# Attention and a two-layer MLP on one core: the first scores of batch 1 set between two begun blocks, and the last 128 tokens stored by column pieces on two queues

## The chip, the cores and the metric

One core of one Trainium2 chip. The metric is the device time of one execution in microseconds (us).

Names: PE is TensorE's matmul unit, PEld its weight loads, DVE is VectorE, ACT ScalarE, POOL GpSimd, SP SyncE. A q behind a name is that engine's sequencer. PSUM is the memory that matmuls write, in banks. A DMA is a transfer between memories; an engine issues it, and here it has landed when its semaphore, a counter that other instructions wait for, has its full count in the trace.

## The reference

```python
q, k, v: (8, 12, 448, 64)                      # batch, heads, tokens, head size, float32
attn = softmax(q @ k^T / 8) @ v                # per head
x    = attn.transpose(0, 2, 1, 3).reshape(3584, 768)
h    = leaky_relu(x @ w_in, 0.01)              # 768 -> 2048
out  = h @ w_out                               # 2048 -> 768, float32, 11 MB
```

## The kernel before

Heads are worked in pairs; HP = 6 pairs make one batch. The first batch's six pairs are the opening. In the main loop, PE alternates between MLP blocks of batch i and attention clusters of later batches. A turn lies between the two: it begins two blocks of the first MLP layer (`part` for m = 0 and 1) with the four pairs of heads that are done, and finishes them when the last pairs are transposed.

```python
def part(i, m, kks, bank=None):        # some of the 6 matmuls of one 128x384 block of x @ w_in
    ...
    for kk in kks:
        nc.tensor.matmul(open_t[m][:, :n], w_in_sb[:, kk, ts(m, P)], xT[:, kk, at:at + n],
                         start=(fresh and kk == kks[0]), stop=(kk == KD - 1))

def pv(u, j, bank=None):               # 16 matmuls of one head, then on DVE:
    ...
    nc.vector.reciprocal(rec, ps[:SC, :, D:])
    nc.vector.tensor_mul(x_t[u][:, :, j, :], ps[:SC, :, :D], rec.to_broadcast([SC, NSC, D]))

# the turn
a, b = idle_slot()                     # two PSUM banks of the scores' pool
part(0, 0, range(4), a)
part(0, 1, range(4), b)
x_transposes(HP - 2)                   # 4 PE transposes of x, then a DVE copy to xT
scores(HP, 0)                          # 2 matmuls, one per head, 64 rows each
expo(HP, 0)                            # exponential on ACT
scores(HP, 1)
expo(HP, 1)
part(0, 0, (4,))
part(0, 1, (4,))
pv(HP - 1, 0)
pv(HP - 1, 1)
scores(HP, 2)
expo(HP, 2)
x_transposes(HP - 1)
transposes(HP + 1)                     # 8 PE transposes of q and k
...                                    # mlp(0) begins with part(0, 0, (5,)) and part(0, 1, (5,))

# the second MLP layer, for each 128 tokens c and each half w of the 768 columns
for m in range(MD):                    # 16 matmuls of 384 columns
    nc.tensor.matmul(ps[:, :NW], h[:, m, ts(c, P)], w_out_sb[:, m, ts(w, NW)], ...)
nc.vector.tensor_copy(o[c][:, ts(w, NW)], ps[:, :NW])
if w == 1:
    store(o.pop(c), cuts[i] + c * P)   # the last 128 tokens: 16 rows, then 112 rows, both by SyncE
```

The softmax here doesn't subtract the row's maximum and nothing guards it: scores larger than these inputs give would overflow.

## Time and profile before

| | before |
|---|---|
| time, median of three runs | 419.16 us (418.84, 419.16 and one of 1447.26) |
| span of the profiled execution | 416.76 us |
| opening: up to the first block matmul of the turn | 26.48 us |
| turn: from there to the first of the last block matmuls | 5.273 us |
| middle: from there to the end of the last matmul | 379.98 us |
| end: from there to the end of the span | 5.02 us |

The four stretches add up to the span. They are taken from the start and end times of PE's instructions in the trace; a matmul's end is modelled, which does not matter where the same instruction is compared. The profile lines of the turn and of the end are in the prediction.

### The profile page before, as it was taken

How to read it: one execution, taken by the hardware profiler on the slowest of the kernel's cores; microseconds unless marked ns; L12 is line 12 of the kernel's file. 1: busy time of each engine (PE TensorE's matmuls, PEld its weight loads, DVE VectorE, ACT ScalarE, POOL GpSimd, SP SyncE). 2: the span in 40 equal slices, each digit the busy share in tenths (PEclk: the TensorE clock that was granted, in tenths of full speed). 3: DMA queues.
4: the chain of work that ended last, by engine and by line, in shares of the span. 5: the costliest groups of instructions: out<-in, count | busy, mean ns of one | idle time of the engine just before them, and what ended most of it. 6: DMA issues, size and time to landing. Idle time of an engine off the chain costs nothing.

```text
span 416.8 us, 8966 instructions
## 1 busy us (share of the span) xinstructions
PE 407.5 (98%) x3742; PEld 235.2 (56%) x3742; DVE 103.5 (25%) x294; ACT 228.9 (55%) x324; POOL 105.1 (25%) x177
## 2 busy tenths in 40 slices
PE   7999999999999999999999999999999999999995
PEld 2566665544656665654565656554465656654562
DVE  3652433211223113320232212221132212310021
ACT  5988872567434774476633684467643486214200
POOL 8876655311112213130311311131130100000000
PEclk9999999999999999999999999999999999999999
DMA  9999999981666848594466947767365521130022
GB/s 137 192 202 203 202 200 122 213 196 40 177 173 172 173 107 187 138 213 110 115 161 175 203 103 188 184 153 185 91 157 137 125 43 24 50 88 0 0 77 76
DMA packets 96265, 57.23 MB, mean 137 GB/s; under 512 B 53216, under 2 KB 92640, under 8 KB 96224
## 3 DMA queue, kind: packets, MB, share of 16 engines
q1 hardware_dynamic: 76592, 44.17, 43.8%
q0 software_dynamic: 19392, 12.26, 20.5%
q8 instruction: 29, 0.48, 0.5%
q10 hardware_dynamic: 240, 0.23, 0.2%
q14 instruction: 12, 0.10, 0.1%
HBM read 45.61 MB, written 11.01 MB: 136 GB/s over the span
## 4 chain that ended last, share of the span: by engine, by line
PE 95%; DVE 2%; DMA 1%; issue 0%; POOLq 0%
PE mm L343 35%; PE mm L314 35%; PE pv L258 13%; PE sc L237 10%; PE tr L222 2%; DMA fq<-in_q_dram 1%; DVE x L266 1%; PE tr L279 1%; PE sc L314 1%; DVE o L347 0%; DVE qkT L226 0%; DVE rec L265 0%; PE mm L177 0%; DVE qkb L137 0%; DVE xT L280 0%
## 5 line engine op out<-in xcount | busy, mean ns | idle before, releaser
L246 ACT ACTIVATE e<-sc 112x896 bf16<-112x896 f32 x192 | 164.7, 915 | 100.8 <-PE sc L237 100.4
L343 PE MATMUL mm<-w_out_sb,h 128*128 128x384 bf16 x896 | 150.2, 326 | 0.5 <-DVE x L266 0.2
L314 PE MATMUL mm<-xT,w_in_sb 128*128 128x512 bf16 (+1 forms) x756 | 148.6, 353 | 0.2 <-DVE x L266 0.2
L343 PEld LDWEIGHTS <-h 128*128 128x128 bf16 x896 | 85.9, 98 | 55.5 <-issue 0.5
L314 PEld LDWEIGHTS <-w_in_sb 128*128 128x128 bf16 x768 | 72.9, 98 | 66.2 <-issue 1.2
L329 ACT ACTIVATE h<-mm 128x512 bf16<-128x512 f32 (+1 forms) x126 | 68.7, 545 | 58.7 <-PE mm L314 58.6
L258 PEld LDWEIGHTS <-e 112*128 112x128 bf16 x1536 | 56.5, 98 | 25.6 <-issue 16.5
L139 POOL CAST v<-fv 112x512 bf16<-112x512 f32 x30 | 18.5, 616 | 194.0 <-PE pv L258 181.7
L258 PE MATMUL pv<-v,e 112*128 112x65 bf16 x1536 | 65.2, 194 | 0.0
L347 DVE COPY o<-mm 128x384 f32<-128x384 f32 x56 | 31.2, 557 | 133.9 <-PE mm L343 133.9
L265 DVE RECIPROCAL rec<-pv 112x4 f32<-112x4 f32 x96 | 17.5, 182 | 150.1 <-PE pv L258 149.6
L237 PE MATMUL sc<-qkT 64*128 64x448 bf16 x384 | 49.8, 357 | 0.7 <-DVE qkT L226 0.7
L266 DVE TENSOR_TENSOR x<-pv,rec 112x256 bf16<-112x256 f32 x96 | 40.7, 424 | 3.3
L237 PEld LDWEIGHTS <-qkT 64*128 64x128 bf16 x384 | 13.8, 94 | 18.8 <-issue 9.9
L137 POOL CAST qkb<-fq 112x512 bf16<-112x512 f32 x30 | 18.4, 613 | 1.8 <-issue 1.2
L137 POOL CAST qkb<-fk 112x512 bf16<-112x512 f32 x30 | 18.4, 613 | 0.9 <-DMA fk<-in_k_dram 0.8
L139 POOL COPY v<-fv 112x512 bf16<-112x512 bf16 x17 | 10.4, 617 | 10.4 <-DMA fv<-in_v_dram 5.7
L137 POOL COPY qkb<-fq 112x512 bf16<-112x512 bf16 x14 | 8.7, 620 | 12.3 <-DMA fq<-in_q_dram 12.3
L226 DVE COPY qkT<-tr 128x896 bf16<-128x896 bf16 (+1 forms) x15 | 8.8, 588 | 11.2 <-PE tr L222 11.2
L137 POOL COPY qkb<-fk 112x512 bf16<-112x512 bf16 x14 | 8.7, 618 | 4.3 <-DMA fk<-in_k_dram 4.3
L222 PE MATMUL tr<-ident,qkb 112*128 112x112 bf16 x112 | 8.8, 225 | 0.3 <-DVE qkb L137 0.3
L222 PEld LDWEIGHTS <-qkb 112*128 112x128 bf16 x112 | 7.2, 103 | 2.7 <-ACT qkb L188 0.6
(30 smaller groups left out, 51.6 us busy)
## 6 DMA issues: line engine op xcount, KB each, us to landing
fk<-in_k_dram SPq DMA_DIRECT2D x31, 224.0 KB, 3.4
fq<-in_q_dram SPq DMA_DIRECT2D x30, 224.0 KB, 3.2
fv<-in_v_dram SPq DMA_DIRECT2D x30, 224.0 KB, 3.8
w_in_sb<-in_moe_w_in_dram POOLq DMA_DIRECT2D x4, 768.0 KB, 11.7
w_out_sb<-in_moe_w_out_dram POOLq DMA_DIRECT2D x4, 768.0 KB, 13.6
out_dram<-o SPq DMA_DIRECT2D x8, 336.0 KB, 3.3
out_dram<-o SPq DMA_DIRECT2D x8, 288.0 KB, 2.6
out_dram<-o SPq DMA_DIRECT2D x8, 240.0 KB, 3.4
```

Source lines behind the costliest of these rows:

```text
L137: by(qk_sb[u][:, x].rearrange("p so h d -> p h so d"), f)
L139: by(v_sb[u % NV][:, :, :, :D], f)
L222: nc.tensor.transpose(tr[:, i, ts(so, SC)], qk_sb[u][:, i, so], ident[:SC, :SC])
L237: nc.tensor.matmul(ps[:, j, :S], t[j * D:(j + 1) * D, S + c * SC:S + c * SC + P], t[j * D:(j + 1) * D, :S], start=True, stop=True,)
L246: nc.scalar.activation(e[:, :, c, :], sc_t.pop((u, c))[:SC, :, :S], AX.Exp, scale=scale)
L258: nc.tensor.matmul(ps[:, qc, :], e[:, at:at + P], vt[:, j, c, :], start=(c == 0), stop=(c == NSC - 1),)
L265: nc.vector.reciprocal(rec, ps[:SC, :, D:])
L266: nc.vector.tensor_mul(x_t[u][:, :, j, :], ps[:SC, :, :D], rec.to_broadcast([SC, NSC, D]))
L314: nc.tensor.matmul(open_t[m][:, :n], w_in_sb[:, kk, ts(m, P)], xT[:, kk, at:at + n], start=(fresh and kk == kks[0]), stop=(kk == KD - 1),)
L329: nc.scalar.activation(h[:, m, :n], open_t.pop(m)[:, :n], AX.Prelu, alpha=0.01)
L343: nc.tensor.matmul(ps[:, :NW], h[:, m, ts(c, P)], w_out_sb[:, m, ts(w, NW)], start=(m == 0), stop=(m == MD - 1),)
L347: nc.vector.tensor_copy(o[c][:, ts(w, NW)], ps[:, :NW])
```

## The change

Its intent: in the turn, put matmul work into the waits for VectorE; at the end, make the last transfer small and issue its two parts side by side.

```diff
--- before.py
+++ after.py
@@ -280,15 +280,16 @@
         nc.vector.tensor_copy(dst, tr[:, 0, :])
 
 
-    def store(o, t0):
-
+    def store(o, t0, cols=slice(0, DM), queues=(nc.sync, nc.sync)):
+
+        queues = list(queues)
         done = 0
         while done < P:
             b, j = divmod(t0 + done, S)
             so, p = divmod(j, SC)
             n = min(SC - p, P - done)
             dst = out[b * S:(b + 1) * S].rearrange("(p so) n -> so p n", so=NSC)
-            nc.sync.dma_start(out=dst[so, p:p + n], in_=o[done:done + n, :])
+            queues.pop(0).dma_start(out=dst[so, p:p + n, cols], in_=o[done:done + n, cols])
             done += n
 
 
@@ -330,24 +331,32 @@
             settle()
             yield KD * n
 
-        todo = [(c, w) for c in range(n // P) for w in range(2)]
+        halves = [slice(0, NW), slice(NW, DM)]
+        todo = [(c, w) for c in range(n // P) for w in halves]
         if i == 0:
-            todo.sort(key=lambda cw: cw[1])
+            todo.sort(key=lambda cw: cw[1].start)
+        if i == B - 1:
+
+            todo[-1:] = [(c, slice(w, w + NW // 2)) for c, w in ((n // P - 1, NW), (n // P - 1, NW + NW // 2))]
         o = {}
         for c, w in todo:
             settle()
             if c not in o:
                 o[c] = o_pool.tile([P, DM], F32, name="o")
             ps = ps_g.tile([P, 4 * P], F32, name="mm", tag="g")
+            nw = w.stop - w.start
             for m in range(MD):
                 nc.tensor.matmul(
-                    ps[:, :NW], h[:, m, ts(c, P)], w_out_sb[:, m, ts(w, NW)],
+                    ps[:, :nw], h[:, m, ts(c, P)], w_out_sb[:, m, w],
                     start=(m == 0), stop=(m == MD - 1),
                 )
-            nc.vector.tensor_copy(o[c][:, ts(w, NW)], ps[:, :NW])
-            if w == 1:
-                store(o.pop(c), cuts[i] + c * P)
-            yield MD * NW
+            nc.vector.tensor_copy(o[c][:, w], ps[:, :nw])
+            t0 = cuts[i] + c * P
+            if i == B - 1 and c == n // P - 1:
+                store(o[c], t0, w, (nc.scalar, nc.sync))
+            elif w.stop == DM:
+                store(o.pop(c), t0)
+            yield MD * nw
 
 
     def supply(u):
@@ -430,19 +439,19 @@
 
     a, b = idle_slot()
     part(0, 0, range(4), a)
-    part(0, 1, range(4), b)
-    x_transposes(HP - 2)
     scores(HP, 0)
     expo(HP, 0)
+    x_transposes(HP - 2)
     scores(HP, 1)
     expo(HP, 1)
-    part(0, 0, (4,))
-    part(0, 1, (4,))
     pv(HP - 1, 0)
     pv(HP - 1, 1)
+    part(0, 1, range(4), b)
     scores(HP, 2)
     expo(HP, 2)
     x_transposes(HP - 1)
+    part(0, 0, (4,))
+    part(0, 1, (4,))
     transposes(HP + 1)
     load_w()
     cast(HP + 3)
```

## The prediction

> **What bounds the kernel now.** I read the page first, for the engine that bounds it and for the chain that ended last; then the timeline at the two places that the diff touches; then the DMA view of the end.
>
> ```profile
> PE 407.5 (98%) x3742; PEld 235.2 (56%) x3742; DVE 103.5 (25%) x294; ACT 228.9 (55%) x324; POOL 105.1 (25%) x177
> PE 95%; DVE 2%; DMA 1%; issue 0%; POOLq 0%
> ```
>
> TensorE (PE) is busy for 407.5 of 416.8 us and carries 95% of the chain. So a change that adds and removes hardly any matmul work can only win what PE spends waiting, and what lies before its first and after its last matmul. There are some 9 us of that in all. The first place is the turn from the six opening heads to the main loop (around 26 to 32 us). The second is the end, after the last matmul (412 to 417 us).
>
> The turn, PE and then VectorE (DVE); columns are start, length, engine, line, operation, and in brackets the idle time before it:
>
> ```profile
> 28.08 0.55 PE L237 MATMUL sc<-qkT 64*128 64x448 bf16 x4
> 28.63 0.48 PE L314 MATMUL sc<-xT,w_in_sb 128*128 128x384 bf16 x2
> 28.95 1.19 PE L258 MATMUL pv<-v,e 112*128 112x65 bf16 x32
> 30.07 0.36 PE L237 MATMUL sc<-qkT 64*128 64x448 bf16 x2
> 30.91 0.37 PE L279 MATMUL tr<-ident,x 112*128 112x112 bf16 x4 [0.47 <-DVE x L266]
> 31.11 0.56 PE L222 MATMUL tr<-ident,qkb 112*128 112x112 bf16 x8
> 31.76 0.48 PE L314 MATMUL sc<-xT,w_in_sb 128*128 128x384 bf16 x2
> ...
> 30.22 0.17 DVE L265 RECIPROCAL rec<-pv 112x4 f32<-112x4 f32 x1
> 30.43 0.42 DVE L266 TENSOR_TENSOR x<-pv,rec 112x256 bf16<-112x256 f32 x1
> 31.31 0.39 DVE L280 COPY xT<-tr 128x448 bf16<-128x448 bf16 x1 [0.46 <-PE tr L279]
> ```
>
> After the pv matmuls PE has only one pair of score matmuls to do, then waits until VectorE has normalised both heads (x done at 30.85) before it can transpose x at 30.91. Then it waits again, for the copy of that transpose (done at 31.70), before the last part of the first block at 31.76.
>
> The end:
>
> ```profile
> 411.78 0.56 DVE L347 COPY o<-mm 128x384 f32<-128x384 f32 x1 [2.04 <-PE mm L343]
> 412.36 0.78 SPq L291 DMA_DIRECT2D out_dram<-o  x2
> out_dram<-o SPq DMA_DIRECT2D x1, 336.0 KB, 2.9
> out_dram<-o SPq DMA_DIRECT2D x1, 48.0 KB, 1.7
> ```
>
> The last copy ends at 412.34, SyncE issues first the 16-row store, then (at 412.72) the 112-row store, which takes 2.9 us from issue to landing, so it lands at 415.64. From there to the end of the span are 1.12 us of closing semaphores, which no diff line touches.
>
> **What the Trainium skill says.** "DMA: Bandwidth & Descriptors", section "Anatomy of one DMA", puts a fixed cost of about 2.0 us on a DMA, mostly the write receipt, with bytes on top. Measured here: 48 KB (16 rows) in 1.74 us, 336 KB in 2.92; so the fixed part is a little smaller than the page has it, and the size does matter. The same page, "Issuing engines are not separate DMA queues": issuing from several engines saves only the issue time. This trace has no overlapping stores to check it with; that saving is one SyncE issue, 0.36 us (412.36 to 412.72). "Perfetto Trace Analysis", "DMA Instruction — HWDGE", says that the descriptor generator is shared and locked during an issue: two engines that issue at once may still take turns. Before, ACT and SP never issue at the same time, so nothing shows it. "VectorE: DVE Perf Modes", in the section on the TRN2 errata, gives a copy out of PSUM a fixed part plus columns over 0.96 GHz: 384 columns are 0.400 us of the measured 0.558, which leaves 0.158 fixed.
>
> **The turn, step by step.** The built order before, from 26.48 us (first matmul of the two opened blocks): 8 block matmuls, 4 transposes of x, 2 pairs of scores, 2 block matmuls, 32 pv, 1 pair of scores, 4 transposes of x, 8 transposes of q and k, last block matmuls. After: 4 block, 1 pair, 4 transposes, 1 pair, 32 pv, 4 block, 1 pair, 4 transposes, 2 block, 8 transposes, last block matmuls. The same instructions; only their order moves.
> Durations, start to start in the timeline where nothing waits: block matmul 0.162 (8 from 26.48 to 27.78); 4 transposes then scores 0.29 (27.78 to 28.08), 4 transposes then anything else 0.20; a pair of scores 0.20 before another pair and 0.27 before anything else (three pairs take 0.67 at 34.52); 32 pv 1.12; 8 transposes 0.40.
> Before without waits: 1.30 + 0.29 + 0.47 + 0.32 + 1.12 + 0.27 + 0.20 + 0.40 = 4.37, so the last block matmuls could start at 30.85. They start at 31.76: 0.9 us is waiting. Piece by piece that is about 0.07 at 28.63 (for the copy that ended at 28.575), 0.57 at 30.91, 0.25 at 31.76. The page's bracket shows less (0.47) since it counts from the modelled end of the pipelined matmul.
> After without waits: 0.65 + 0.27 + 0.29 + 0.27 + 1.12 + 0.65 + 0.27 + 0.20 + 0.32 + 0.45 = 4.49: 0.12 more, for one more change from scores to other work and one more step. That ends at 30.97.
> Are the waits really gone? Scores first: qkT was copied by 26.27, its PSUM buffer freed by the exponential that ends at 26.86; PE comes at 27.13. First transposes of x: x done at 27.32, PE comes at 27.40. Second scores: buffer free at 27.67, PE at 27.69. Transposes after pv: pv ends at about 29.28; reciprocals and multiplies (0.18 and 0.42 each, two heads overlapped as before) end near 30.0; PE now has 0.65 of block matmuls and 0.27 of scores to do first and comes at 30.05. The last block matmuls: copy done near 30.84, PE at 30.97, because 2 block matmuls and 8 transposes lie between instead of 8 transposes alone. All pass, three of them by less than 0.1 us. So the most is 31.76 - 30.97 = 0.79; I take 0.7.
> Does it last? The page shows PE at 9 or more tenths from there on, and the waits on the chain are for VectorE, so they shift along with PE. The weight chunks that the next block matmuls need landed at 28.40 and 35.36 by the trace, with PE asking for them at 35.2 and about 43. The q and k casts that the next transposes need are, at the tightest, done at 48.07 for a transpose at about 49.7; 0.8 us earlier still fits. I count all of it.
>
> **The end, step by step.** The last 16 matmuls of 384 columns become 32 of 192. Start to start, 384 columns take 0.1625; half should be near 0.081 (weights load faster than that: pv runs at 0.035 with a weight load each). The last matmul is shorter in the pipeline. Estimate: PE ends 0.02 later.
> Copy of the last piece: 0.158 + 192/960 = 0.36 in place of 0.56: 0.20 earlier.
> The 112-row store is issued first on its own queue: 0.36 earlier.
> It moves a quarter of the bytes. Landing from issue: 16 rows (1 packet an engine) 1.74, 112 rows (7 packets of 3072 B an engine) 2.92, so six more packets cost 1.18 less the wait behind the first store, some 0.15 to 0.2 each. At 768 B I estimate 0.06 to 0.1 each (the trace has 1024 B packets at 0.046 to 0.068 and 3072 B at 0.121 in the middle): landing 2.1, so 0.8 saved.
> Sum: 0.20 + 0.36 + 0.80 - 0.02 = 1.34. I take 1.3. The earlier pieces, 192 and 96 KB, leave about 2.6 and 1.3 us before the last, and are nearly through by then.
>
> **Rivals.** (a) The turn gives little: knife-edge checks fail, PE waits for x before the transposes as before; then 0.3 instead of 0.7, and 417.5 in all. For it: three margins under 0.1 us; against it: 0.92 us of other work now lies where there was 0.27. (b) The two queues take turns at the descriptor generator, and the small store on ACT goes first: the issue gain of 0.36 goes, 417.4. (c) The receipt dominates and size hardly counts: landing stays near 2.6, 0.5 lost, 417.6. Against it: the landing at the end grows with rows, 1.8 (32), 2.6 (96), 2.9 (112). (d) The turn's gain is swallowed by a load further on: then 417.8. Against it: the slack figures above. (e) 192-column matmuls are bound by weight loads, at 0.1 each: 0.6 us more, 417.7. The pv pace speaks against it.
>
> **Range and chances.** 419.16 - 0.7 - 1.3 = 417.16; the two undisturbed runs average 419.0, which would make it 417.0. I say 417.1. If only the end pays, 417.9; if everything pays in full and the small packets are faster than I think, 416.5. Range 416.3 to 418.0. Two per cent is 8.4 us, four times the whole gain, and nothing that the diff adds could cost as much: within 2% at 0.98.
>
> **What would show it.** In the changed profile: no bracket for x before the transposes near 30 us, the last block matmuls at about 31.0 instead of 31.76, every later PE event, up to the last matmul (411.7 before), 0.7 earlier; a last copy of 128x192 at 0.36 us; the last 112-row store issued right after it (about 0.03 us) and landing in about 2.1 us; the span at 414.8. It is wrong if PE still idles at the second transposes, if the shift at 60 us is gone by 400 us, if the last store waits for the ACT issue, or if the store lands in 2.6 us or more.

## The result, and the profile after

In the first comparison the changed kernel took 416.4 us (median of 6 runs, 415.91 to 416.8), the kernel before 419.0 (median of 6). The ratio is 0.9937, with a 95% interval of 0.9916 to 0.9957. A ratio is the mean time of one kernel's fast runs over that of the other's of the same rounds, so it is not quite the ratio of the two medians. Executions over 1.5% slower than the fastest of the same kernel are left out of the means. In a later comparison the same kernel took 416.64 us (0.9942, 0.9927 to 0.9956). The median of 416.4 lies inside the predicted range, 0.7 below the point, and the change is within the 2% that the prediction expected it to stay under.

| stretch, us | before | after | difference |
|---|---|---|---|
| opening | 26.48 | 26.15 | -0.33 |
| turn | 5.273 | 4.647 | -0.63 |
| middle | 379.98 | 380.03 | +0.05 |
| end | 5.02 | 3.56 | -1.46 |
| span | 416.76 | 414.39 | -2.37 |

Timeline of PE in the changed kernel's turn, and then of DVE (start, length, engine, line, operation, count, idle time before it):

```profile
26.15 0.81 PE L315 MATMUL sc<-xT,w_in_sb 128*128 128x384 bf16 x4
26.90 0.36 PE L237 MATMUL sc<-qkT 64*128 64x448 bf16 x2
27.19 0.37 PE L279 MATMUL tr<-ident,x 112*128 112x112 bf16 x4
27.50 0.36 PE L237 MATMUL sc<-qkT 64*128 64x448 bf16 x2
27.79 1.20 PE L258 MATMUL pv<-v,e 112*128 112x65 bf16 x32
28.83 0.81 PE L315 MATMUL sc<-xT,w_in_sb 128*128 128x384 bf16 x4
29.57 0.36 PE L237 MATMUL sc<-qkT 64*128 64x448 bf16 x2
29.87 0.37 PE L279 MATMUL tr<-ident,x 112*128 112x112 bf16 x4
30.08 0.49 PE L315 MATMUL sc<-xT,w_in_sb 128*128 128x384 bf16 x2
30.41 0.56 PE L222 MATMUL tr<-ident,qkb 112*128 112x112 bf16 x8
30.80 0.49 PE L315 MATMUL sc<-xT,w_in_sb 128*128 128x384 bf16 x2
```

```profile
29.28 0.42 DVE L266 TENSOR_TENSOR x<-pv,rec 112x256 bf16<-112x256 f32 x1
30.28 0.39 DVE L280 COPY xT<-tr 128x448 bf16<-128x448 bf16 x1 [0.57 <-PE tr L279]
```

No PE line has an idle bracket any more. x is ready at 29.70 and PE comes for it at 29.87; the copy ends at 30.67 and PE needs it at 30.80. The two waits of before have gone.

The changed kernel's end, from its timeline, and then from its DMA view (out<-in, engine, count, KB each, us from issue to landing):

```profile
409.55 0.36 DVE L353 COPY o<-mm 128x192 f32<-128x192 f32 x1 [0.76 <-PE mm L349]
410.87 0.36 DVE L353 COPY o<-mm 128x192 f32<-128x192 f32 x1 [0.96 <-PE mm L349]
411.25 0.32 SPq L292 DMA_DIRECT2D out_dram<-o  x1
411.26 0.38 ACTq L292 DMA_DIRECT2D out_dram<-o  x1
```

```profile
out_dram<-o SPq DMA_DIRECT2D x1, 168.0 KB, 2.4
out_dram<-o SPq DMA_DIRECT2D x2, 84.0 KB, 1.8
out_dram<-o ACTq DMA_DIRECT2D x2, 12.0 KB, 2.0
```

The last copy is 0.20 us shorter. Both last stores are issued 0.03 us after it, 4 ns apart, and SyncE's takes no longer to issue than the 16-row store of before did (0.316 against 0.315). SyncE's 112 rows land after 1.77 us in place of 2.92, ScalarE's 16 rows after 1.94.

The opening is the same code in both kernels, instruction for instruction on PE, and it is not part of the effect. In the fourteen profiles it ends anywhere from 26.15 to 31.66 us. In three of them (27.23, 27.82 and 31.66) the granted clock drops in it. From the windows view (stretch, length, busy time of PE, PEld, DVE, ACT and POOL with counts, granted clock, DMA share, GB/s), before, then the changed kernel run again (opening 27.82), then an experiment (31.66):

```profile
0.00:12.00 12.00, 9.74 (x56) 3.88 (x56) 4.04 (x24) 6.84 (x10) 8.43 (x17) 1.00 0.97 140
12.00:26.00 14.00, 13.26 (x221) 8.86 (x220) 9.79 (x29) 13.90 (x19) 12.85 (x21) 1.00 1.34 201
```

```profile
0.00:12.00 12.00, 8.73 (x48) 3.36 (x49) 3.72 (x23) 6.63 (x9) 8.50 (x17) 0.81 0.96 138
12.00:26.00 14.00, 13.37 (x212) 8.71 (x209) 8.85 (x26) 13.03 (x17) 12.31 (x20) 0.91 1.34 201
```

```profile
0.00:12.00 12.00, 9.38 (x43) 3.46 (x44) 3.34 (x23) 6.46 (x9) 8.50 (x17) 1.00 0.98 138
12.00:26.00 14.00, 11.84 (x151) 7.18 (x148) 9.18 (x19) 9.60 (x12) 12.64 (x21) 0.88 1.34 201
```

The column before the last two shows it: 1.00 and 1.00, then 0.81 and 0.91, then 1.00 and 0.88. The clock explains part of the spread at most, since the eleven openings at full clock already range from 26.15 to 27.23 us. What sets the rest was not settled. It is why a difference of 0.3 us between two times says nothing here, while the turn (4.645 to 4.647 in all ten profiles of the new order) repeats to a few ns and the end of the same code to some 0.03 us.

### The profile page after: what moved, and what is told of

Same layout as the page of the kernel before. It is cut to its first block, busy times and chain, and to the rows that moved or that the text cites. A ratio compares the mean times of both kernels' runs of the same rounds, so it can differ in the third digit from the quotient of the medians.

```text
span 414.4 us, 9008 instructions
## 1 busy us (share of the span) xinstructions
PE 405.9 (98%) x3758; PEld 235.8 (57%) x3758; DVE 104.0 (25%) x295; ACT 228.9 (55%) x324; POOL 105.6 (25%) x177
## 4 chain that ended last, share of the span: by engine, by line
PE 95%; DVE 2%; DMA 1%; ACT 1%; issue 0%; POOLq 0%
PE mm L349 35%; PE mm L315 35%; PE pv L258 13%; PE sc L237 10%; PE tr L222 1%; DMA fq<-in_q_dram 1%; ACT e L246 1%; PE tr L279 1%; DVE x L266 1%; PE sc L315 0%; DVE o L353 0%; DVE qkb L137 0%; DVE rec L265 0%; DVE qkT L226 0%; POOLq L498 0%
## 5 line engine op out<-in xcount | busy, mean ns | idle before, releaser
L349 PE MATMUL mm<-w_out_sb,h 128*128 128x384 bf16 (+1 forms) x912 | 150.2, 323 | 0.5 <-DVE x L266 0.2
L349 PEld LDWEIGHTS <-h 128*128 128x128 bf16 x912 | 87.0, 98 | 54.6 <-issue 0.5
L353 DVE COPY o<-mm 128x384 f32<-128x384 f32 (+1 forms) x57 | 31.4, 551 | 133.5 <-PE mm L349 133.5
```

What stands on the lines that cost most here:

```text
L349: nc.tensor.matmul(ps[:, :nw], h[:, m, ts(c, P)], w_out_sb[:, m, w], start=(m == 0), stop=(m == MD - 1),)
L353: nc.vector.tensor_copy(o[c][:, w], ps[:, :nw])
```

## The experiments

Theory: the turn and the end give their gains independently. The turn gains because block matmuls fill the waits for VectorE. The end gains mostly because the last packets are small, and partly because the second issue is not behind the first. All runs were correct. Times of the kernel before in the three calls: 418.97 (11 runs), 418.91 (7) and 419.41 (11).

| run | median us | ratio, 95% interval | opening | turn | end |
|---|---|---|---|---|---|
| turn_only | 418.19 | 0.9982 (0.9949 to 1.0015) | 26.60 | 4.646 | 5.01 |
| store_only | 417.40 | 0.9949 (0.9923 to 0.9975) | 26.66 | 5.280 | 3.55 |
| one_queue | 417.61 | 0.9958 (0.9929 to 0.9987) | 27.23 | 4.646 | 3.95 |
| rows_two_queues | 418.15 | 0.9970 (0.9943 to 0.9998) | 27.08 | 4.646 | 4.77 |
| scores_first_only | 419.26 | 1.0014 (0.9986 to 1.0043) | 26.77 | 5.675 | 5.01 |
| blocks_later_only | 417.82 | 0.9973 (0.9956 to 0.9989) | 26.66 | 4.692 | 4.99 |
| swap_queues | 416.33 | 0.9965 (0.9906 to 1.0024) | 31.66 | 4.646 | 3.29 |
| narrow_last | 416.97 | 0.9957 (0.9936 to 0.9978) | 26.74 | 4.646 | 3.74 |
| changed_again | 416.64 | 0.9942 (0.9927 to 0.9956) | 27.82 | 4.645 | 3.54 |
| lane_shift | 416.66 | 0.9939 (0.9924 to 0.9955) | 26.81 | 4.646 | 3.32 |
| lane_shift_swap | 416.67 | 0.9933 (0.9920 to 0.9946) | 26.68 | 4.645 | 3.50 |
| halves_only | 417.84 | 0.9969 (0.9952 to 0.9986) | 27.23 | 4.645 | 4.10 |

### Each half of the change alone

turn_only is the kernel before with the new turn; store_only is the changed kernel with the old turn.

> The kernel before with the turn's new order alone. Theory: the turn stretch (first block matmul to the first of the last block matmuls) is 4.65 us as in the changed kernel, against 5.27 before; the stretch from the last matmul's end to the span's end stays 5.0 us; the time is 0.6 us under before (ratio 0.9985). Rival 1 (the 0.33 us by which the changed kernel's opening, up to 26.15 against 26.48 us, ran earlier belongs to the change): the opening ends near 26.15 again and the gain is 0.95. Rival 2 (the turn's gain is given back later): the turn is 4.65 but the last matmul ends no earlier than the opening explains.

> The changed kernel with the turn's old order. Theory: turn 5.27 us; from the last matmul's end to the span's end 3.56 us as in the changed kernel, against 5.02 before; time 1.4 us under before (ratio 0.9966). Rival: turn and store share their gain (sum of the two single parts clearly off 2.0 us).

Measured: turn 4.646 with an end of 5.01; turn 5.280 with an end of 3.55. Each part gives its own gain and leaves the other's stretch alone. The middle is 379.99 and 380.02, so nothing is given back. The opening ended at 26.60 and 26.66, not at 26.15: the 0.33 us does not belong to the change. The times agree (0.75 and 2.1 us by the ratios), with intervals too wide to weigh 0.6 us.

### Which part of the turn's new order does it

scores_first_only moves only the scores; blocks_later_only moves only the blocks. Both start from the kernel before.

```diff
 # scores_first_only                      # blocks_later_only
 part(0, 0, range(4), a)                   part(0, 0, range(4), a)
 part(0, 1, range(4), b)                  -part(0, 1, range(4), b)
+scores(HP, 0); expo(HP, 0)                x_transposes(HP - 2)
 x_transposes(HP - 2)                      scores(HP, 0); expo(HP, 0)
-scores(HP, 0); expo(HP, 0)                scores(HP, 1); expo(HP, 1)
 scores(HP, 1); expo(HP, 1)               -part(0, 0, (4,)); part(0, 1, (4,))
 part(0, 0, (4,)); part(0, 1, (4,))        pv(HP - 1, 0); pv(HP - 1, 1)
 pv(HP - 1, 0); pv(HP - 1, 1)             +part(0, 1, range(4), b)
 scores(HP, 2); expo(HP, 2)                scores(HP, 2); expo(HP, 2)
 x_transposes(HP - 1)                      x_transposes(HP - 1)
                                          +part(0, 0, (4,)); part(0, 1, (4,))
```

> The kernel before with only the first scores of batch 1 (and their exponential) moved ahead of the transposes of x; the opened blocks' matmuls stay where they were. Theory (the gain comes from matmul work moved into the waits for VectorE): the waits for x before the second transposes and for their copy stay, and the turn stretch is 5.2 to 5.35 us. Rival (the gain comes from the exponentials' earlier start on ScalarE): 4.7 us or less.

Measured: 5.675, worse than before by 0.40 and worse than I expected. Its timeline, PE then DVE:

```profile
28.16 0.36 PE L237 MATMUL sc<-qkT 64*128 64x448 bf16 x2
28.46 0.37 PE L279 MATMUL tr<-ident,x 112*128 112x112 bf16 x4
28.76 0.36 PE L237 MATMUL sc<-qkT 64*128 64x448 bf16 x2
29.31 0.48 PE L314 MATMUL sc<-xT,w_in_sb 128*128 128x384 bf16 x2 [0.19 <-DVE xT L280]
...
31.59 0.37 PE L279 MATMUL tr<-ident,x 112*128 112x112 bf16 x4 [0.47 <-DVE x L266]
```

```profile
28.86 0.39 DVE L280 COPY xT<-tr 128x448 bf16<-128x448 bf16 x1 [1.26 <-PE tr L279]
```

The wait at 31.59 has stayed. A new one has come at 29.31: with one pair of scores taken from behind the transposes, only one pair covers the copy from 28.86 to 29.25. This wait costs some 0.18 us more than the short one that stood at this place before. The rest of the 0.40 is work: eight block matmuls take 1.396 us before scores and 1.300 before transposes, and the two pairs with the transposes between them take about 0.13 us more than side by side. An earlier exponential did not help.

> The kernel before with only the block matmuls moved: the second block's four behind pv, the last one of each behind the second transposes; the scores stay behind the first transposes. Theory: the long waits are gone, but PE now comes to the first transposes 0.25 us before x is ready; two changes from scores to other work fewer give back 0.2: turn stretch about 4.7 us. Rival (early exponentials): 5.2 or more, since the exponentials start 0.5 us later than in the changed kernel.

Measured: 4.692 against 4.7 expected. The gain comes from the block matmuls, 0.58 of the 0.63 us. The scores' new place is worth 0.05 us on top: it hides the wait for x that blocks_later_only still has at its first transposes (four block matmuls take 0.65 us, the transposes start 0.90 us after the first of them):

```profile
26.66 0.81 PE L314 MATMUL sc<-xT,w_in_sb 128*128 128x384 bf16 x4
27.56 0.37 PE L279 MATMUL tr<-ident,x 112*128 112x112 bf16 x4
```

### Pieces or queues

one_queue issues all pieces by SyncE; rows_two_queues keeps the two queues and drops the pieces; halves_only stores two halves of 384 columns on the two queues.

```diff
 # one_queue
-store(o[c], t0, w, (nc.scalar, nc.sync))
+store(o[c], t0, w)
 # rows_two_queues: no cut into quarters, and for the last 128 tokens, after the second half
+store(o.pop(c), t0, slice(0, DM), (nc.scalar, nc.sync))
 # halves_only: todo[-1:] is not replaced by two quarters
```

> The changed kernel with all column pieces issued by SyncE, 16 rows first. Theory: the 112-row piece is issued 0.36 us later and lands 1.8 us after that, so 2.2 us after the last copy instead of 1.97: 0.2 us longer than the changed kernel. Rival (the second queue carries the gain of the end): it loses 0.36 us or more, and up to the whole 1.3.

> The changed kernel without column pieces: the last 128 tokens are stored as whole rows of 3072 B, 16 rows by ScalarE's queue and 112 by SyncE's. Theory: the last copy is 0.56 us again, the 112 rows land 2.6 to 2.8 us after their issue, so the stretch from the last matmul's end to the span's end is 4.4 to 4.6 us: 0.9 to 1.0 longer than the changed kernel's 3.56. Rival (the queue carries the gain): 3.8 or less.

> The changed kernel with the last 128 tokens stored in two halves of 384 columns on the two queues, the second half not cut again. Theory: copy 0.56 us (0.20 more), packets of 1536 B land about 2.25 to 2.4 us after their issue, closing after the landing near 1.05 since these two stores have later places in the list: 3.9 to 4.05 us from the last matmul's end to the span's end. Rival (the cut into quarters is not needed once the first half is out early): 3.6 or less.

Measured from the last matmul's end: 3.95, 4.77 and 4.10, against 5.02 before and 3.56 changed. The pieces without the queue give 1.07 us of the 1.46; the queue gives 0.25 without the pieces and 0.39 on top of them. All three expectations were off. one_queue's loss of 0.39 lies by its letter in the rival's range (0.36 or more, expected 0.2), though the queue does not carry the gain. I had set the delay of the 112 rows against the later landing of ScalarE's 16 rows, which turned out not to gate the end (next part but one); the 112 rows landed 2.19 us after the copy, 0.39 later than in the changed kernel, and that is the whole loss. The 1.07 is net of 0.24 us that the pieces lose in the closing waits (next part but one). In the other two the 112 rows landed later than I thought. The DMA views of rows_two_queues and of halves_only (the second's medians take in the first half too):

```profile
out_dram<-o SPq DMA_DIRECT2D x1, 336.0 KB, 3.0
out_dram<-o ACTq DMA_DIRECT2D x1, 48.0 KB, 2.8
```

```profile
out_dram<-o SPq DMA_DIRECT2D x2, 168.0 KB, 2.4
out_dram<-o ACTq DMA_DIRECT2D x2, 24.0 KB, 2.2
```

The 16 rows took 1.74 us ahead of the others on SyncE's queue in the kernel before; on ScalarE's queue beside the 112 rows they take 2.76. By the trace's packet records their packets start 0.51 us after the first of the 112 rows' and take 0.16 us each (median) against 0.12. This fits two queues that share what moves the data, but the queue of the 16 rows changed too, so it is not shown apart. Landing of the last 112 rows by SyncE, with 16 rows beside them on the other queue: 1.77 us with packets of 768 B, 2.49 with 1536 B, 3.03 with 3072 B. The bytes of the store grow with the packets here, so the runs do not tell these two apart.

### A still narrower last piece

```diff
-todo[-1:] = [(c, slice(w, w + NW // 2)) for c, w in ((n // P - 1, NW), (n // P - 1, NW + NW // 2))]
+todo[-1:] = [(n // P - 1, slice(NW, DM - P)), (n // P - 1, slice(DM - P, DM))]   # 256 and 128
```

> The changed kernel with the last half cut into 256 and 128 columns in place of 192 and 192. Theory: the last copy takes 0.158 + 128/960 = 0.29 us in place of 0.36, the last matmul is 0.03 shorter in the pipeline, the landing stays within 0.1 of 1.93: 0.1 us shorter at the end, unless matmuls of 128 columns with a weight load each are slower than 0.056 us apart. Rival (the piece before it is now still in flight and delays the last): the landing takes 2.1 or more and the gain is gone.

Measured: the copy took 0.29 us as expected, yet the end is 3.74, which is 0.17 longer. The gain is gone, as the rival said. The stores of the piece before are issued only 0.73 us before the last copy ends (1.29 in the changed kernel) and land 1.27 and 1.53 us after it (0.51 and 0.78). The last stores, though smaller, landed after 2.01 (112 rows) and 2.20 us (16 rows). That the piece before it delays the last one was not shown apart from the smaller packets (512 B).

### Exchanged queues, and a find in the closing

```diff
-store(o[c], t0, w, (nc.scalar, nc.sync))
+store(o[c], t0, w, (nc.sync, nc.scalar))
```

> The changed kernel with the queues exchanged: 16 rows by SyncE, 112 rows by ScalarE. In the changed kernel the 16 rows on ScalarE's queue landed 1.93 us after issue, later than the 112 rows on SyncE's (1.77). If the queue makes that difference: 112 rows land 1.95 or more after issue and 16 rows 1.65. If the number of rows or packets does: 112 rows 1.75 to 1.8 and 16 rows 1.9.

Measured: 112 rows by ScalarE 1.79, 16 rows by SyncE 1.51: neither account fits both. The end is 3.29, 0.27 shorter than the changed kernel's, though the later landing moved only from 1.97 to 1.83 us after the copy. What follows the landing had shortened too. So I read SyncE's last instructions in the trace's records one by one; no view prints them. Before the program ends, SyncE waits for eight DMA semaphores one after the other, always in the order 108, 112, 113, ..., 118. Times in us after the end of the last copy:

```
                 stores, semaphore: landing      SyncE's waits pass at                               span ends
before           16 rows 114: 1.76               108 1.24 ... 114 1.78, 115 3.32, 116 3.38, 118 3.50     4.42
                 112 rows 115: 3.30
changed          112 rows (SP) 108: 1.80         108 1.82, 112 1.89, 113 1.95 ... 117 2.19, 118 2.25     3.17
                 16 rows (ACT) 118: 1.97
swap_queues      16 rows (SP) 108: 1.54          108 1.56, 112 1.63, 113 1.69 ... 117 1.93, 118 1.99     2.90
                 112 rows (ACT) 118: 1.83
lane_shift       16 rows (ACT) 117: 1.93         108 0.47, 112 0.53 ... 116 0.78, 117 1.95, 118 2.01     2.93
                 112 rows (SP) 118: 1.77
```

In the changed kernel the store that holds semaphore 108 comes last but one to land, and the other seven waits, 0.06 us each, all stand behind it. ScalarE's later landing is hidden in the row. In swap_queues the store with 108 is the small one, and it lands early. From this came a new theory: the place of the last stores' semaphores in the list counts. A store fewer moves both to its end.

```diff
 # lane_shift: of the last half, the 16 rows are stored once, 384 columns, with the last piece
-store(o[c], t0, w, (nc.scalar, nc.sync))
+a, b = nc.scalar, nc.sync
+if w.stop < DM and w.start > 0:
+    store(o[c], t0, w, (None, b))                                        # 112 rows alone
+else:
+    store(o[c], t0, [slice(w.start // NW * NW, w.stop), w], (a, b))      # columns of each store
 # lane_shift_swap: a, b = nc.sync, nc.scalar
```

> The changed kernel once more, unedited, for the same chip and rounds as the three below. Turn 4.65 us and 3.56 us from the last matmul's end to the span's end, as before; what differs from run to run is the opening, up to the first block matmul (26.15 to 31.7 us in the runs so far).

> The changed kernel with one store fewer: the 16 rows of the last half go out together, 384 columns at the end, in place of 192 and 192. Theory: SyncE's closing list waits for eight DMA semaphores in a fixed order, 0.06 us each; in the changed kernel the last 112-row store has the first one of the list, so all the others come after it (landing of that store to the span's end 1.37 us). With five stores the last two have the last two places: from the later landing to the span's end 1.0 us, landing itself unchanged near 1.97, so 3.35 to 3.4 us from the last matmul's end in place of 3.56. Rival (the place in the list does not matter): 3.55 or, since the 16 rows now have packets of 1536 B, more.

> The same with the queues exchanged (16 rows by SyncE, 112 by ScalarE). Theory: landing 1.83 us after the last copy as in the earlier exchange of queues, the closing 1.0: 3.2 to 3.25 us from the last matmul's end to the span's end, against 3.29 with the exchange alone. Rival: 3.3 or more.

changed_again repeated turn (4.645) and end (3.54). lane_shift: the landing is 1.93 us after the copy, nearly as in the changed kernel, and 0.99 remain after it: 3.32 in all, 0.22 less than changed_again. The theory of the list held. The last lines of its timeline show copy and issue unchanged:

```profile
411.52 0.36 DVE L356 COPY o<-mm 128x192 f32<-128x192 f32 x1 [0.96 <-PE mm L352]
411.91 0.32 SPq L295 DMA_DIRECT2D out_dram<-o  x1
411.91 0.38 ACTq L295 DMA_DIRECT2D out_dram<-o  x1
```

lane_shift_swap missed: after the landing 0.99 remain, as expected, but ScalarE's 112 rows landed only 2.12 us after the copy (1.83 in swap_queues), and the end is 3.50. Whether the 16 rows' wider packets beside it delayed it was not tested; this stays open. lane_shift's and swap_queues' ends, 3.32 and 3.29, are the shortest; each stands on one profile. lane_shift's time (416.66) cannot be told from that of the changed kernel (416.64) with these runs.

## Why the prediction was right

By its own steps:

**The bound.** PE carries 95% of the chain in both kernels. Only the turn and the end moved, as said.

**The turn's waits.** Right: all are gone, also the three checks with less than 0.1 us to spare, and the block matmuls are the part that does it (4.692 alone). There was some luck in the narrow checks: x was ready 0.20 and 0.17 us before PE came for it, where 0.08 and 0.05 were forecast, in part because the block matmuls before the scores took longer than assumed (next step).

**The turn's sum.** Forecast 4.49 us of work, measured 4.647; so 0.63 us gained in place of at most 0.79, close to the 0.7 that was taken. The mis-sized term is the step from full-height block matmuls to a pair of scores on 64 rows each. The forecast used 0.65 us for four block matmuls whatever follows. With scores behind them they take 0.746, twice: 0.19. Scores to other work took 0.295 in place of 0.27, three times: 0.08. On the other side, 32 pv took 1.04 in place of 1.12, since the 1.12 of before included a step to scores of this kind, and the eight transposes took 0.05 less than assumed. With three smaller differences of 0.01 each, that makes the 0.16 missed.

**It lasts.** Right: the middle is 379.98 before and 380.03 after, of which 0.04 is the split of the last 16 matmuls.

**The end.** Forecast 1.34, measured from the first matmul of the last half 1.41 (7.78 before, 6.37 after). By its terms, with what gates the end, the 112-row store:

| term | forecast | measured |
|---|---|---|
| last matmuls | +0.02 | +0.04 |
| last copy | -0.20 | -0.20 |
| issue no longer behind the other | -0.36 | -0.36 |
| landing of the 112 rows, from issue | -0.80 | -1.14 |
| closing after that landing | 0 | +0.25 |
| sum | -1.34 | -1.41 |

Two terms were wrong and nearly cancelled, so it is in part luck that the sum came so close. The packets were quicker than estimated: by the trace's packet records the last ones of 768 B take 0.036 us each (median), where the prediction took 0.06 to 0.1. "1.12 us of closing semaphores, which no diff line touches" was false: the diff changed the number of stores, and so which place in the closing list the last one has; 1.37 us follow its landing in place of 1.12. That ScalarE's 16 rows would land last was not foreseen either; it cost nothing, because their semaphore stands last in the list.

**The rivals.** (a), a wait for x: none in the trace. (b), turns at the descriptor generator: the two issues start 4 ns apart and take 0.316 and 0.377 us. SyncE's took 0.315 without one beside it, so the gain of 0.36 stands. ScalarE may pay a little: its store of 112 rows took 0.323 us to issue when none was beside it and 0.373 beside one of SyncE (both in lane_shift_swap). The second queue is worth 0.39 us with the pieces and 0.25 without, about the one SyncE issue of 0.36 that the prediction set for it. (c), landing hardly depends on size: 1.77, 2.49, 3.03 speak against it. (d), the gain swallowed later: the middle says no. (e), the 192-column matmuls slowed by weight loads: they start 0.0825 us apart.

**The time.** The stretches that the change touches give 2.04 us (0.63 + 1.41), the prediction took 2.0, and the ratios of the two comparisons give about 2.6 and 2.4, with intervals that hold 2.0. The excess has the size of the openings' spread; it was not traced run by run.

## What to carry to other kernels

When an engine is full but for a few waits, find what it waits for and put independent work of about that length there, counting the steps between kinds of matmul as work of their own. At the end of a kernel, cut the last store so that the final piece is small and the piece before it has time to land, and count landing, issue and closing waits one by one: a second queue gave 0.25 us alone here and 0.39 on top of small pieces, small pieces alone 1.07. Judge gains of a few tenths of a us by stretches of the trace that repeat, not by the time of a run whose opening varies by several us.

## What the Trainium skill lacked or had wrong

- The nearest page, "Runtime: NRT & Kernel Launch", has a closing barrier over the engines, but no page that was read describes a program's closing waits for its DMAs. Here SyncE waited for eight DMA semaphores one by one, 0.06 us each, in an order that does not follow the landings; the place of the last store in it changed the end by 0.22 us (3.54 against 3.32).
- "DMA: Bandwidth & Descriptors", "Anatomy of one DMA": its fit of 2.0 us plus bytes over 436 GB/s is for DMAs issued by GpSimd, which the prediction did not say; carried over, it gives an estimate of 2.2 us for 84 KB and 2.8 for 336 KB. For these stores by SyncE, each with 16 rows on the other queue beside it, the runs show 1.77 and 3.03 (packets of 768 and 3072 B): a smaller fixed part and a larger slope.
- "Perfetto Trace Analysis", "DMA Instruction — HWDGE", lets an issue wait while another holds the descriptor generator, which is locked for exclusive use, and gives no time for that wait. Two issues 4 ns apart on SyncE and ScalarE took 0.316 and 0.377 us. The only such wait that these runs leave room for is ScalarE's 0.05 us (0.373 beside an issue of SyncE, 0.323 alone), far less than an issue; that it is the lock is not shown.
- "TensorE: Matmul & The Clock Gate", "Back-to-back issue gap", gives about 131 ns a matmul at N = 512 in streams with a weight load each, and says that N/2.4 + 2.5 over-counts there. In the trace of before, 24 such matmuls of 512 columns take 5.18 us, 216 ns each; 384 and 192 columns take 162.5 and 82.5 ns. That formula gives all three.
- "TensorEngine Tiling (Array Packing)", "Key Properties", names a drain when the tiling mode changes, but no page that was read gives the time of a step from matmuls on 128 rows to matmuls on 64. Here it is 0.10 us more than to a transpose: 0.746 against 0.65 us for four of the former.
